# New orders of work in five places: a linear-attention and expert-mixture kernel on one core

## The chip, the cores and the metric

The kernel runs on one core of one Trainium2 chip. A core has TensorE (PE: matmuls, with its weight loads shown apart as PEld), VectorE (DVE), ScalarE (ACT), GpSimd (POOL) and SyncE (SP). The engines run side by side, each in the order of its own list of instructions, and wait for one another through semaphores. In this kernel POOL issues the loads from the inputs, and SP issues transposing DMAs, stores and reloads. The metric is the device time of the whole program in microseconds, as the median of several runs. For this kernel a difference of under 0.2% can't be told from none.

## The reference

Inputs are q, k, v (8 batches, 8 heads, 576 positions, 64 features) and a layer of 8 experts over 4608 tokens of 512 features.

```python
# attention, per batch and head
r = maximum(x, 0); phi(x) = concat(r * cos(pi/2 * pos/S), r * sin(pi/2 * pos/S))
kv = phi(k)^T @ v;  z = sum over positions of phi(k)
x = (phi(q) @ kv) / (phi(q) @ z + 1e-6)          # tokens x 512
# routing: 8 rounds of Sinkhorn on exp(x @ w_gate - max)
P /= P.sum(1) + 1e-9;  P /= P.sum(0) + 1e-9;  P *= N / E
# experts
out = sum over e of P[:, e] * (maximum(x @ w1[e], 0) @ w2[e])
```

All tokens go through all experts, so the work is almost all matmuls: x by w1 (512 x 1024) and the hidden layer by w2 (1024 x 512), eight times.

## The kernel before, in words

**Two phases.** In the first, attention of batch after batch is made in between the matmuls of expert 0. In the second, experts 1 to 7 run over six units of 768 tokens each (two halves of 384), with Strassen's scheme of seven products for both layers.

**The written order.** `te`, `ve` and `se` (class `InOrder`) tie each instruction of TensorE, VectorE and ScalarE to the one issued before it on the same engine, so that these engines follow the program's text. From the end of the first unit on `ve`, and from expert 2 on `se`, is the free engine, and the scheduler may move what is not tied.

**First phase.** Expert 0 works in blocks `j` of 512 tokens with 16 slots each: slots 0 to 7 are `ffn1` (one of eight column tiles of w1, four matmuls of 512 columns), slots 8 to 15 are halves of `ffn2`. The table `todo`, filled by `at(block, slot, fn, ...)`, says which attention step stands behind which slot. Block `j` carries attention of batch `j + 1` and the preparing of batch `j + 2`. A batch has four head pairs `hk`, loaded in two halves:
- `load`: q, k, v from memory, on POOL's queue;
- `prep_q`: q times cos and sin on VectorE; for batches 0 and 1 `turn` transposes it on TensorE, from batch 2 on a transposing DMA on SP does;
- `prep_k` is the Relu of k, `prep_kp` its product with cos and sin, `prep_v` the copy of v beside a column for z;
- `sums` makes kv and z on TensorE and copies them out; `denominators` makes the divisors and, on VectorE, their reciprocals `hl`;
- `spread_out` (copies `rb` on ACT) and `numerators` (products on VectorE) write `xT`; `attend` is both;
- `gates` makes exp of the routing logits, `P_tok`.

Batch 0 has no expert work beside it: it is written out by hand ahead of the blocks, with `keep_busy` matmuls on constants as fillers. It ends in the first four column tiles of block 0, whose four k tiles are interleaved with the attention's head pairs.

**Between the phases.** Blocks 7 and 8 of expert 0 have no attention. There the Sinkhorn rounds are made by the generator `sinkhorn`, five steps per round: row sums and reciprocal; scaling and column sums `colp`; two of the expert's weight sums (`tw_steps`); a matmul of `colp` with ones on TensorE and further weight sums; reciprocal and scaling. `balanced(n)` takes n steps. Beside it VectorE makes `x_sums`, the Strassen sums of x for a unit (S1, S2, S4 and one in place in `xT`), which are also saved to memory so that later experts reload them with `x_again`. The last block's `ffn2` (`dealt`) is spread as fillers over the first unit of expert 1 (`start_fill`), together with Sinkhorn's last rounds.

**Second phase.** `group` makes one of four column groups of a unit: seven products, with copies on ACT (`Y`, u2, u4, Relu) and additions on VectorE between them, and a call of `fill` behind each. In later units `pair_fill` puts one step of the second layer (`Pair`) there; it also issues `gate`, ScalarE's scaling of one finished tile of expert 0 by its P, for the 36 tiles one by one.

Of the kernel before, what the change touches and what calls it, by code (L numbers as in the profile page):

```python
# [25 lines left out]
def kernel(  # L26
# [128 lines left out]
    def ffn2(hT, w, c0, g, y_ps, fts):  # L155

        for ft in fts:
            te.matmul(
                out=y_ps,
                lhsT=hT[:, ft, c0 : c0 + P],  # L160
                rhs=w[1][:, ft, :],
                start=(ft == 0),
                stop=(ft == FT - 1),
            )
        if FT - 1 in fts:

            if g % 2 == 0 or g < (B - 1) * TCH // P:
                se.copy(out=acc(g), in_=y_ps)
            else:
                ve.tensor_copy(out=acc(g), in_=y_ps)  # L170

    def store(g, cols=slice(0, Dm), queues=(nc.sync, nc.sync)):
        for half, queue in enumerate(queues):
# [5 lines left out]
            )  # L179

    with ExitStack() as p1:
# [13 lines left out]
        landing = {}  # L195
        sources = {"q": q, "k": k, "v": v}

        def load(b, half, names="qkv", held_back=False):
            for name in names:
# [6 lines left out]
                if held_back:  # L206
# [10 lines left out]
        load(0, 0, "q")  # L217
        gidx = cs_pool.tile([P, C], FP32, name="gidx")
# [4 lines left out]

        ones_sq = cs_pool.tile([P, P], F16, name="ones_sq")
# [6 lines left out]
        load(0, 1, "q")  # L231
        for name in "kv":
            load(0, 0, name)
            load(0, 1, name)
# [22 lines left out]
        for _ in range(74):  # L257
            keep_busy(1)
# [17 lines left out]
        for hh in range(2):  # L276
            ve.tensor_copy(
                out=cs_half[hh * HP : (hh + 1) * HP, :, :, hh],
                in_=cs[hh * HP : (hh + 1) * HP, :, :, 0],
            )  # L280
# [8 lines left out]
        C3 = C // 3  # L289

# [6 lines left out]
        with nc.allow_low_precision("sums of zeros and ones"):  # L297
# [11 lines left out]
        ones_col = const.tile([P, 1], FP32, name="ones_col")  # L309
        ve.memset(ones_col[:], 1.0)  # L310
        ones_all = const.tile([P, P], FP32, name="ones_all")
        ve.memset(ones_all[:], 1.0)
        eps_row = cs_pool.tile([1, 32], FP32, name="eps_row")
        ve.memset(eps_row[:], 1e-6 / XS)
# [8 lines left out]
        lent = acc_lo[:, G_LO - 4 : G_LO, :].rearrange("p g d -> p (g d)").bitcast(F16)  # L323
        VA = C * (D + 2)
        v_augs = [
            lent[:, i * VA : (i + 1) * VA].rearrange("p (c d) -> p c d", d=D + 2)
            for i in range(4)
        ]
# [7 lines left out]
        for t in v_augs:  # L336
            ve.memset(t[:, :, D : D + 1], 1.0 / XS)

# [7 lines left out]
        def prep_q(b, hk):  # L346
# [12 lines left out]
            if by_dma:  # L359
# [5 lines left out]
                if b == 3 and hk == 0:  # L365

                    after(landing["v", b, 1], turned)
            else:
# [77 lines left out]
        def sums_begun(b, half):  # L446
# [7 lines left out]
            kv_ps = [ps_s.tile([P, 512], FP32, name="small_ps") for hh in range(2)]  # L454
# [157 lines left out]
        for hk in range(HK):  # L612
            if hk == 3:
# [3 lines left out]
                prep_q(0, hk)  # L617
                key_sums_made(0, z_ps)
            else:
                prep_q(0, hk)  # L620
            for i in range(3):
                turn(0, hk, i, True)
                keep_busy(3)
        prep_kp(0, 0)
        prep_kp(0, 1)
        denominators(0, range(0, 4))
        keep_busy(8)
        for hk in (2, 3):
            prep_k(0, hk)
        z_ps = key_sums(1)  # L630
        prep_kp(0, 2)
        key_sums_made(1, z_ps)
        prep_kp(0, 3)
        keep_busy(5)
        denominators(0, range(4, 8))
        for half in range(2):
            sums_made(0, half, sums_begun(0, half))
            keep_busy((0, 18)[half])
# [6 lines left out]
        ]  # L645
        for hk in range(HK):
            attend(0, hk)
            for kt in ((), (0,), (1,), (2, 3))[hk]:
                for ft, h_ps in enumerate(first_ps):
                    te.matmul(  # L650
                        out=h_ps[:],
                        lhsT=w0[0][:, kt, ft * P : (ft + 1) * P],
                        rhs=xT[:, kt, 0:TCH],
                        start=(kt == 0),
                        stop=(kt == KT - 1),
                    )
                    if kt == KT - 1:
                        se.activation(out=hT[:, ft, 0:TCH], in_=h_ps[:], func=AF.Relu)
            for i in ((), (0,), (1, 2), ())[hk]:
                prep_k(1, i, i < 2)  # L660
            for i in ((), (0,), (1,), (2, 3))[hk]:
                if i == 3:
                    prep_k(1, i, False)
                prep_kp(1, i)
# [3 lines left out]
        for j in range(B):  # L668
            b = j + 1
            if j == 0:  # L670
# [4 lines left out]
                for hk in range(HK):  # L675
                    for i in range(3):
                        at(0, (5, 6, 6, 7)[hk], turn, 1, hk, i, i != 1)
                    if hk == 0:
                        at(0, 5, prep_q, 1, 3)
                    if hk == 2:  # L680
                        at(0, 6, prep_v, 1, 0, se.copy)
                        at(0, 6, prep_v, 1, 2, ve.tensor_copy)
                    if hk == 3:
                        at(0, 7, prep_v, 1, 1, se.copy)
                        at(0, 7, prep_v, 1, 3, ve.tensor_copy)
# [6 lines left out]
            elif b < B:  # L692
# [14 lines left out]
                elif j == 2:  # L707
                    at(j, 0, sums, b, 1)
# [5 lines left out]
                at(j, 6 if j == 1 else 3 if j == 2 else 4, denominators, b)  # L714
# [567 lines left out]
```

The softmax here doesn't subtract the row's maximum and nothing guards it: scores larger than these inputs give would overflow.

## Time and profile before

| what | us |
|---|---|
| median of 4 runs (977.34 to 979.83) | 978.69 |
| the profiled execution | 977.77 |
| its span, first to last instruction | 976.1 |
| TensorE, VectorE, ScalarE busy | 961.7, 807.9, 564.0 |
| end of batch 0 and first products of block 0 | 24.9 |
| block 1; block 2; blocks 3 to 6 | 44.8; 65.4; 84.5 to 162.1 |
| blocks 7 and 8; first unit of expert 1 | 162.1 to 184.7; to 205.3 |

Times inside the profile are microseconds from the span's start. A line of the timeline has the start, the time, the engine, the line of code, the operation with what it writes and reads, its size and its count, and in brackets how long the engine stood idle before it and for whom. Instructions that were recorded by the helper of `InOrder` all show its line, L109, so they are told apart by the tiles they write. The page shows the granted clock of TensorE as 9 tenths or more in all of its 40 slices.

### The profile page before, as it was taken

To read this page: it belongs to the slowest core of one execution; us is meant where nothing else is said; L and a number is where in the kernel's file an instruction comes from. 1 tells how busy PE (TensorE), PEld (TensorE's weight loads), DVE (VectorE), ACT (ScalarE), POOL (GpSimd) and SP (SyncE) were. 2 spreads that over 40 slices of the span, in tenths; PEclk is the share of its full clock that TensorE was granted. 3 is DMA by queue.
4 is the path that set the end of the run, shared out by engine and by line. 5 is a ranking of instruction groups with operands and counts; after the bars stand their busy time and mean duration, and the time that the engine had idled before them with its cause. 6 is when DMAs were issued, how large, how long until landed. Compare 5 with 4: busy or idle time off the path is not lost.

```text
span 976.1 us, 20236 instructions
## 1 busy us (share of the span) xinstructions
PE 961.7 (99%) x7855; PEld 674.9 (69%) x7855; DVE 807.9 (83%) x1833; ACT 564.0 (58%) x1262; POOL 60.7 (6%) x82
## 2 busy tenths in 40 slices
PE   9999999999999999999999999999999999999997
PEld 6545555457777777777777777777777777777775
DVE  7767775888988987987888987987888887988887
ACT  5766665477776555555555555555555555555551
POOL 6231110010000000000000000000000000000001
PEclk9999999999999999999999999999999999999999
DMA  9999985331104401332103401323103401104435
GB/s 163 188 156 168 158 136 111 68 68 39 37 26 84 77 25 42 66 55 65 33 26 85 77 25 42 63 55 67 34 26 83 78 25 40 35 26 122 126 89 128
DMA packets 80336, 73.54 MB, mean 75 GB/s; under 512 B 33264, under 2 KB 72176, under 8 KB 80240
## 3 DMA queue, kind: packets, MB, share of 16 engines
q0 software_dynamic: 27232, 30.94, 20.4%
q1 hardware_dynamic: 52768, 41.06, 17.3%
q8 instruction: 61, 1.00, 0.4%
q14 instruction: 35, 0.29, 0.1%
q10 hardware_dynamic: 240, 0.26, 0.1%
HBM read 83.12 MB, written 12.98 MB: 98 GB/s over the span
## 4 chain that ended last, share of the span: by engine, by line
PE 88%; DMA 4%; DVE 3%; issue 2%; ACT 1%; POOL 1%; POOLq 0%; ACTq 0%; SPq 0%
PE rows_ps L109 33%; PE h_ps L109 26%; PE p_ps L109 11%; PE copied_ps L109 11%; PE y_ps L109 4%; PE small_ps L109 2%; DMA k_ld<-in_k_dram 1%; DMA w2e<-in_moe_w_dram 1%; DMA w1e<-in_moe_w_dram 1%; DMA acc_hi<-q_p 1%; DVE P_tok L109 1%; DVE colp L109 0%; POOL q_ld L202 0%; DVE rs L109 0%; DVE acc_hi L955 0%
## 5 line engine op out<-in xcount | busy, mean ns | idle before, releaser
L955 DVE SCALAR_TENSOR_TENSOR acc_lo<-rows_ps,P_tok,acc_lo 128x512 f32<-128x512 f32 (+1 forms) x322 | 203.6, 641 | 74.8 <-PE rows_ps L109 74.8
L109 PEld LDWEIGHTS <-H 128*128 128x128 f16 x2080 | 203.1, 98 | 82.5 <-issue 1.2
L891 ACT CAST u<-h_ps 128x384 f16<-128x384 f32 x288 | 137.8, 478 | 131.2 <-PE h_ps L109 131.2
L109 PEld LDWEIGHTS <-w1e 128*128 128x128 f16 x1632 | 157.7, 98 | 67.6 <-issue 5.2
L885 DVE CUSTOM_DVE_ANT_0 H<-p_ps,u 128x384 f16<-128x384 f32 x329 | 181.5, 552 | 6.5 <-PE p_ps L109 6.5
L109 PEld LDWEIGHTS <-hs 128*128 128x128 f16 x1500 | 146.6, 98 | 56.2
L109 PE MATMUL h_ps<-S,w1e 128*128 128x384 f16 x672 | 164.1, 326 | 0.7 <-ACT u L109 0.6
L109 PE MATMUL p_ps<-xT,T 128*128 128x384 f16 x672 | 164.1, 326 | 0.1
L109 PE MATMUL rows_ps<-V,H 128*128 128x256 f16 x1000 | 150.0, 273 | 0.7 <-DVE acc_hi L955 0.7
L109 PE MATMUL rows_ps<-w2e,hs 128*128 128x256 f16 x1000 | 150.0, 273 | 0.0
L109 PE MATMUL h_ps<-xT,w1e 128*128 128x384 f16 (+1 forms) x616 | 148.7, 350 | 0.1
L923 ACT ACTIVATE H<-h_ps 128x384 f16<-128x384 f32 x144 | 70.7, 491 | 95.0 <-PE h_ps L109 95.0
L109 PEld LDWEIGHTS <-T 128*128 128x128 f16 x1008 | 98.4, 98 | 30.1 <-issue 3.6
L109 PE MATMUL rows_ps<-w2e,H 128*128 128x256 f16 (+1 forms) x568 | 92.3, 284 | 0.0
L904 ACT COPY copied_ps<-h_ps 128x384 f32<-128x384 f32 x144 | 67.5, 468 | 35.4 <-PE h_ps L109 35.4
L914 ACT ACTIVATE H<-copied_ps 128x384 f16<-128x384 f32 x144 | 70.9, 492 | 20.3 <-PE copied_ps L109 20.3
L109 PE MATMUL h_ps<-S,T 128*128 128x384 f16 x336 | 81.8, 324 | 0.4 <-ACT copied_ps L109 0.3
L109 PE MATMUL copied_ps<-xT,w1e 128*128 128x384 f16 x336 | 82.1, 326 | 0.0
L109 PE MATMUL copied_ps<-w2e,H 128*128 128x256 f16 x504 | 75.5, 272 | 0.0
L109 PE MATMUL rows_ps<-V,hs 128*128 128x256 f16 x500 | 75.0, 272 | 0.0
L955 DVE SCALAR_TENSOR_TENSOR acc_lo<-copied_ps,P_tok,acc_lo 128x256 f32<-128x256 f32 x126 | 60.3, 478 | 0.6 <-PE copied_ps L109 0.2
L955 DVE SCALAR_TENSOR_TENSOR acc_hi<-rows_ps,P_tok,acc_hi 128x512 f32<-128x512 f32 (+1 forms) x56 | 41.4, 738 | 20.5 <-PE rows_ps L109 19.7
(145 smaller groups left out, 948.8 us busy)
## 6 DMA issues: line engine op xcount, KB each, us to landing
S<-x_saved SPq DMA_DIRECT2D x108, 192.0 KB, 2.4
out_dram<-acc_lo SPq DMA_DIRECT2D x62, 128.0 KB, 2.4
w1e<-in_moe_w_dram POOLq DMA_DIRECT2D x7, 1024.0 KB, 8.7
w2e<-in_moe_w_dram POOLq DMA_DIRECT2D x7, 1024.0 KB, 10.0
q_ld<-in_q_dram POOLq DMA_DIRECT2D x16, 288.0 KB, 6.5
k_ld<-in_k_dram POOLq DMA_DIRECT2D x16, 288.0 KB, 8.2
v_ld<-in_v_dram POOLq DMA_DIRECT2D x16, 288.0 KB, 9.2
x_saved<-S SPq DMA_DIRECT2D x18, 192.0 KB, 1.9
```

Source lines behind the costliest of these rows:

```text
L109: i = getattr(self.engine, name)(*args, **kwargs)
L885: latest = ve._custom_dve(TENSOR_ADD_SAT, out=out, in0=ps[:, 0:TU], in1=t[:], s0=FP32_MAX, s1=0.0)
L891: se.copy(out=t[:], in_=ps[:, 0:TU])
L904: se.copy(out=Y[:, 0:TU], in_=X[:, 0:TU])
L914: se.activation(out=h11, in_=Y[:, 0:TU], func=AF.Relu)
L923: se.activation(out=h12, in_=X[:, 0:TU], func=AF.Relu)
L955: ve.scalar_tensor_tensor(out=a, in0=rows, scalar=P_tok[:, g, self.e : self.e + 1], in1=a, op0=ALU.mult, op1=ALU.add,)
```

## The change

Five edits:
1. **First batch in new order.** The second q load is issued ahead of the position table (iota), k's first half ahead of the identity; small constants are written earlier. The 74 fillers of 128 columns at the start become 110 of 64. All four `prep_q` come before k; `cs_half` is filled after the second; sums, spreads and numerators are written out one by one, the second sums in another bank; the first products follow; k of batch 1 is prepared behind them instead of in between. In block 0 the turns of batch 1 move from slots 5, 6, 6, 7 to 6, 6, 7, 7, and all copies of v go to VectorE.
2. **Fourth batch's sums later.** Batch 3's preparing in block 1 and its sums and denominators take the slots that later batches have: sums in block 2, slot 2 (before: block 1 slot 15 and block 2 slot 0). All its transposes wait for its last v load, and the loads of batch 4 wait for its last transpose. Batch 4's preparing in block 2 is one slot later.
3. **x sums of two units in block 6.** They go into k's and q's buffers at slots 2 and 5, are saved, and are reloaded with `x_again` at the start of the second phase.
4. **Sinkhorn on a table of slots.** The steps of the rounds stand at listed slots and fills; the weight sums are dealt 2, 3, 4, 3, 4 to the rounds; block 7's tiles are all copied by ScalarE; the last block's second layer goes in 8 parts per tile, one in each fill, the last two in the second unit.
5. **Gating in ScalarE's order.** `gate` uses the ordered engine also after expert 1.

```diff
-            if g % 2 == 0 or g < (B - 1) * TCH // P:
+            if g % 2 == 0 or g < B * TCH // P:
                 se.copy(out=acc(g), in_=y_ps)
...
+    def x_sums(n, ts):
...
+        for i, t in enumerate(ts):
+            saved.append(
+                nc.sync.dma_start(out=x_saved[n, i], in_=t.rearrange("p k t -> p (k t)"))
+            )
...
+                if behind is not None:
+                    after(turnings[behind], i)
+                elif held_back:
                     after(ve.last, i)
...
         load(0, 0, "q")
+        load(0, 1, "q")
         gidx = cs_pool.tile([P, C], FP32, name="gidx")
...
+        load(0, 0, "k")
...
-        load(0, 1, "q")
-        for name in "kv":
-            load(0, 0, name)
-            load(0, 1, name)
+        load(0, 1, "k")
+        for half in range(2):
+            load(0, half, "v")
...
-        for _ in range(74):
-            keep_busy(1)
+        for _ in range(110):
+            te.matmul(
+                out=idle_ps[:, 0:HP], lhsT=ones_sq[:],
...
-                if b == 3 and hk == 0:
+                if b == 3:
                     after(landing["v", b, 1], turned)
+                turnings[b, hk] = turned
...
         for hk in range(HK):
+            prep_q(0, hk)
+            if hk == 1:
+                halve()
             if hk == 3:
                 prep_k(0, 0)
                 prep_k(0, 1)
                 z_ps = key_sums(0)
-                prep_q(0, hk)
-                key_sums_made(0, z_ps)
...
+        sums_made(0, 0, sums_begun(0, 0))
+        keep_busy(20)
+        spread_out(0, 0)
+        numerators(0, 0)
+        keep_busy(4)
+        spread_out(0, 1)
+        sums_made(0, 1, sums_begun(0, 1, (ps_h[0], "h_ps")))
...
+        numerators(0, 1)
+        spread_out(0, 2)
+        first_l1(0, (2, 3, 0, 1))
+        numerators(0, 2)
+        spread_out(0, 3)
+        first_l1(1, range(4))
+        numerators(0, 3)
+        prep_k(1, 0)
+        prep_k(1, 1)
+        first_l1(2, range(4))
+        first_l1(3, range(4))
         for hk in range(HK):
-            attend(0, hk)
...
+            if hk >= 2:
+                prep_k(1, hk, False)
+            prep_kp(1, hk)
...
-                        at(0, (5, 6, 6, 7)[hk], turn, 1, hk, i, i != 1)
+                        at(0, (6, 6, 7, 7)[hk], turn, 1, hk, i, i != 1)
...
-                elif j == 2:
-                    at(j, 0, sums, b, 1)
...
-                    (4, prep_q, 0), (5, prep_q, 1), (8, prep_k, 0), (8, prep_q, 2),
-                    (9, prep_k, 1), (10, prep_kv, 0), (10, prep_k, 2), (12, prep_q, 3),
-                    (12, prep_kv, 1), (12, prep_k, 3), (13, prep_kv, 2), (14, prep_kp, 3),
-                    (14, prep_v, 3),
+                    (4, prep_q, 0), (5, prep_q, 1), (9, prep_k, 0), (8, prep_q, 2),
+                    (10, prep_k, 1), (12, prep_q, 3), (12, prep_k, 2), (13, prep_k, 3),
+                    (13, prep_kv, 0), (14, prep_kv, 1),
                 ) if j == 1 else (
-                    (4, prep_q, 0), (5, prep_k, 0), (5, prep_q, 1), (6, prep_k, 1),
-                    (8, prep_q, 2), (8, prep_k, 2), (10, prep_q, 3), (10, prep_k, 3),
+                    (5, prep_q, 0), (6, prep_q, 1), (8, prep_k, 0), (8, prep_q, 2),
+                    (9, prep_k, 1), (10, prep_q, 3), (10, prep_k, 2), (11, prep_k, 3),
                     (11, prep_kv, 0), (14, prep_kv, 1),
...
-                if j == 1:
-                    at(j, 15, sums, b + 1, 0)
             if j == 1:
                 for name in "qkv":
                     for half in range(2):
-                        at(j, 12, load, b + 2, half, name, True)
+                        at(j, 12, load, b + 2, half, name, True, (b + 1, HK - 1))
...
+        for n in range(2):
+            at(B - 2, (2, 5)[n], x_sums_early, n)
...
-            se.mul(out=acc(g), in_=acc(g), mul=P_tok[:, g, 0:1])
+            bound[2].mul(out=acc(g), in_=acc(g), mul=P_tok[:, g, 0:1])
...
+    tw_steps = [[steps_left.pop(0) for _ in range(n)] for n in (2, 3, 4, 3, 4, 0, 0, 0)]
...
+    for n in range(2):
+        x_again(n, xs_first[n], saved[-1])
...
-            2 if j < NJ - 1 else 4,
+            2 if j < NJ - 1 else 8,
...
-            since = (j - B + 1) * NS + slot - 5
-            if since == -4:
-                balanced(3)
-            elif since >= 0 and since % 5 < 2:
-                balanced((1, 4)[since % 5])
+            balanced({1: 3, 4: 5, 8: 5, 13: 5, 17: 5, 22: 5}.get((j - B + 1) * NS + slot, 0))
...
-        if k_fill % 7 in (0, 2, 3, 5):
+        for _ in range(1 + (k_fill % 14 == 1)):
             next(tiles, None)
-        if k_fill % 6 != 1:
-            balanced(1)
+        balanced({3: 1, 4: 1, 6: 1, 8: 2, 12: 1, 13: 1, 15: 1, 17: 2, 21: 1, 22: 1}.get(k_fill, 0))
...
     def pair_fill():
         nonlocal k_fill, slot2
         k_fill += 1
+        for _ in range(2):
+            next(tiles, None)
```

## The prediction

> **What bounds the kernel now.** I read the page first, for which engine is never idle; then busy time by stage, for where TensorE stops being full; then TensorE's waits and its timeline in those stages; then the engine each wait names.
>
> ```profile
> PE 961.7 (99%) x7855; PEld 674.9 (69%) x7855; DVE 807.9 (83%) x1833; ACT 564.0 (58%) x1262; POOL 60.7 (6%) x82
> ...
> 44.80:65.40 20.60, 20.28 (x213) 9.77 (x213) 17.11 (x38) 14.49 (x32) 4.30 (x6) 1.00 1.02 149
> 65.40:84.50 19.10, 17.87 (x198) 9.23 (x198) 12.27 (x29) 12.49 (x29) 5.47 (x8) 1.00 1.16 187
> 84.50:162.10 77.60, 77.60 (x834) 40.17 (x833) 53.86 (x123) 48.41 (x113) 13.41 (x19) 1.00 0.88 144
> 162.10:184.70 22.60, 22.57 (x127) 10.77 (x126) 17.86 (x47) 10.90 (x20) 0.00 (x0) 1.00 0.15 53
> 184.70:205.30 20.60, 17.31 (x93) 8.73 (x92) 15.59 (x37) 12.01 (x25) 3.87 (x3) 1.00 0.31 52
> 308.70:400.00 91.30, 91.30 (x701) 68.30 (x699) 76.87 (x170) 51.04 (x115) 0.88 (x1) 1.00 0.20 45
> ```
>
> The columns are PE, PEld, DVE, ACT, POOL, clock, DMA share, GB/s. TensorE bounds the kernel, so nothing can be gained where it is full: from 84.5 to 162 and after 308. Busy time hides short stops, because matmuls overlap; so I measure a stop as start to next start, less what the same matmuls take undisturbed (0.216 us for 512 columns, 0.163 for 384). From 308 to 955 that excess is about 0.01 us per 10 us. It is found in four places before that: the first 35 us, blocks 1 and 2 (56 to 73), the Sinkhorn stretch (176 to 200), and the unit behind it (200 to 210). The change touches all four.
>
> ```profile
> PE copied_ps L109 <- DVE colp L109: 3.0, 4, 1.2
> PE h_ps L109 <- ACT u L109: 0.6, 2, 0.3
> PE h_ps L109 <- ACT copied_ps L109: 0.3, 1, 0.3
> ```
>
> **Sinkhorn on a table of slots (-4.3).** Eight times a small product of column sums stands in TensorE's order and waits for VectorE's `colp`:
>
> ```profile
> 184.99 0.59 PE L109 MATMUL rows_ps<-w2e,H 128*128 128x512 f16 x2
> 186.78 0.39 PE L109 MATMUL copied_ps<-colp,ones_all 128*128 128x8 f32 x2 [1.19 <-DVE colp L109]
> 187.03 0.48 PE L109 MATMUL h_ps<-S,T 128*128 128x384 f16 x2
> ```
>
> Two matmuls of 0.43 take 1.79 here: 1.36 lost. By the same subtraction the third to eighth products lose 0.19, 0.14, 1.36, 0.47, 0.91 and 0.90, which is 3.97; and each of these six takes 0.24 where the two unhurried ones take 0.14, so 0.6 more. Loss: 4.6.
>
> One iteration costs VectorE, from the rows between 168.13 and 170.94 (reciprocal, scale, row sums, reciprocal, scale, column sums), 2.81; with 0.32 from the product to the reciprocal it can repeat every 3.2 us. Before, it is slower because VectorE's order also holds four weight sums (about 0.25 each), rows copies (0.69) and the x sums of two units (four of 0.55 each). The table puts the products of blocks 7 and 8 after slots 4, 8, 13, 17 and 22: 4 or 5 slots of 4 x 0.216, so 3.6 us or more. Between slot 22 and fill 3 stand one slot, the mark and 11 matmuls: 0.87 + 0.22 + 2.07 + 0.14 = 3.3. After that 9 fills of 0.54 (two of 384 columns, one of 512), so 4.9. All are over 3.2, the third by only 0.1. The weight sums now fall into the gaps left by the wider slots; the first two stand at slot 1 (166), and their weights, issued at 147.74, land 8.2 us later, so in time. Block 7's copies go to ACT, which was idle 1.13 and 3.00 us before the two it had (171.6, 175.2). Eight parts, two left for the next unit and other banks are the same matmuls: 0. One matmul per fill leaves 0.76 us between two accumulations in a bank; the copy between 190.98 and 191.75 fits that without a stop. I keep 0.3 for the narrow gap: -4.3. Ends: -4.6, and -1 if VectorE still comes half a microsecond late seven times.
>
> **x sums in block 6 (0).** Two times four additions of 0.56, 2.2 us each, go to VectorE at slots 2 and 5. VectorE is busy 53.86 of 77.60 in blocks 3 to 6, and 3.1 us idle before the numerators at 160.25. After the sums (147.1 on this trace) the first ends at 149.5, before the denominators' 149.8; the second runs from 152.3 to 154.5, before the numerators at 155.1. Uncovered it would cost 0.3 to 1.5. New DMA: six stores and six loads of 192 KB on SP (1.9 to 2.4 us each, 0.15 DMA share in that stage), needed first at 185. Behind them on SP nothing is due.
>
> **Gates in ScalarE's order (-0.6).** Four gates of expert 2's unit were free to move, and landed here, between the copies that TensorE waits for:
>
> ```profile
> 202.15 0.73 ACT L1107 ACTIVATE acc_lo<-acc_lo,P_tok 128x512 f32<-128x512 f32 x1
> 203.19 0.72 ACT L1107 ACTIVATE acc_hi<-acc_hi,P_tok 128x512 f32<-128x512 f32 x1
> ```
>
> TensorE loses 0.21, 0.44, 0.44, 0.46 and 0.11 from 201.8 to 210, 1.66 in all. In the new order they are gone from there; one copy of 0.59 now stands before the copy of h_ps in the second group, which I price at 0.3. So -1.35. But the order lists three of the four together in expert 2's first group, between the copy of h_ps and u2: 3 x 0.64 start to start, so u2 is ready at 3.05 us behind the first product where TensorE wants it at 2.3 to 2.75. That is +0.3 to +0.75; I take 0.75. The 0.35 us that each later unit of expert 1 loses has the same gates behind it and stays. Ends: -1.7 and +0.8.
>
> **Fourth batch later (-2.4).**
>
> ```profile
> 58.43 0.46 PE L109 MATMUL small_ps<-hl,acc_hi 96*128 96x192 f16 x3 [0.19 <-ACT rb L109]
> ...
> 67.38 0.46 PE L109 MATMUL small_ps<-acc_lo,k_p 64*128 64x65 f16 x18 [0.31 <-DVE acc_lo L109]
> 68.04 0.46 PE L109 MATMUL small_ps<-acc_lo,k_p 64*128 64x65 f16 x18 [0.21 <-DVE k_p L109]
> ...
> 72.52 0.34 PE L109 MATMUL small_ps<-acc_hi,zsel 128*32 128x192 f16 x6 [0.71 <-DMA acc_hi<-q_p]
> ```
>
> The first stop (0.35 + 0.29) is ACT standing in order on a Relu of k that waits for its load (idle 1.33 before 56.84); the Relu moves one slot back, behind the rb copies. The next two (0.48 + 0.37) are the fourth batch's sums, asked for before VectorE has made k_p and v; they go to slot 2 of block 2. The last (0.88) is a transposing DMA issued at 65.92, while the next batch's loads were issued from 65.87 on; it landed after 6.6 us, where (4,3) took 3.3. Sum 2.37. As a check, block 2 then has the written order of blocks 3 to 6, whose period is 19.0 without stops.
>
> New waits: the four transposes wait for the last v load (63.0; about 60.4 without transposes among the loads and with the shift below). Behind them on SP stand only transposes; for them waits TensorE's denominator product at 69.5. One each 1.35 us from 60.4, the last landing by 68.5: in time. The six loads of batch 4 then wait for that landing; behind them on POOL stand only later loads. Issue at 68.1, first landing 4.7 later (as 83.34 to 88.10), then 1.45 each: 72.8 to 80. VectorE wants the first at about 73, since its use moves from slot 4 to 5.
> A rule weighed here: the Trainium skill, "DMA: Bandwidth & Descriptors", section on queues, rings and completion order, has each engine go round its queues packet by packet. By it, holding loads back gains no bandwidth and only shifts them, 2.2 us later: with no slack at 73 that is +2 against -0.9, a net of -0.4 here. By the row, 6.6 against 3.3, the transpose gets its 3.3 back and the loads run 1.45 apart, undisturbed. I go by the row, and keep -0.4 as the end.
>
> **First batch in new order (-0.8).**
>
> ```profile
> 10.86 0.76 DVE L109 TENSOR_TENSOR q_p<-q_ld,acc_hi 128x1152 f16<-128x1152 f16 x1
> 12.02 1.42 DVE L109 TENSOR_TENSOR k_p<-k_ld,acc_hi 128x1152 f16<-128x1152 f16 x2
> 15.45 1.35 DVE L109 RECIPROCAL den<-y_ps 96x192 f32<-96x192 f32 x1
> 18.49 0.82 DVE L109 TENSOR_TENSOR xT<-small_ps,rb 128x384 f16<-128x384 f32 x2 [0.94 <-ACT rb L109]
> ```
>
> POOL: the second q load moves ahead of iota (issue 2.62 to 2.07), the tables 0.8 later (4.29 to 5.05), still before VectorE's 6.0. Landings run one per 1.45 from 8.94 on, so the stream gains 0.3. From k's landing (10.4) to the reciprocal VectorE ran 5.05: now the fourth q_p (0.7) fills the wait for k, and one k_p (0.7) goes behind, so the reciprocal starts at 14.2 and hl ends at 16.4 for 17.54. Spreads, products and copies follow as before with the second sums (0.6) among them: first products of block 0 end at 23.9 for 24.91. But the k_p that filled VectorE's waits between now come after: from 22.85 on 9.5 us of VectorE work without a gap (four k_p of 0.68, two Relu 0.33, four q_p 0.69, four turns 0.5, four v copies 0.37) to 32.4, and the sums end at 32.9 for 33.72. Fillers stand in TensorE's waits only: 0. So -0.8, and VectorE and the transposes carry it on. Ends: -2 (no refilled waits), +0.5 (w2, which lands until 34.25, or another wait takes it).
> The second rule: the Trainium skill, "TensorE: Matmul & The Clock Gate", Part 1, warns of half clock after an idle window of about 3.4 us. The trace shows the start alone: 74 fillers of 128 columns took 6.36 us, 107 ns apart and later 56. With 110 of 64 columns, half of each row's spacing, that is 5.3 us. The longest stop in my order is 0.9 (before hl), so by the row 0; by the rule too, unless a stop passes 3.4: then 3.4 us at half speed, +1.7.
>
> **Sum.** -0.8 - 2.4 + 0 - 4.3 - 0.6 = -8.1. The span 976.1 becomes 968.0; its execution took 977.77, 1.67 more, so 969.7; the runs' median, 978.69, lies 0.92 higher: 970.6, say 970.5.
>
> **Rivals.** (a) VectorE still comes last in Sinkhorn. For it: 0.1 of slack in one gap and 83% busy; against: the x sums and copies have left. 978.7 - (8.1 - 3.5) = 974. (b) The stops only change place: gates in expert 2 at +0.8, loads at their bad end, narrow slots, no gain at the start. 978. (c) Slower: batch 4's loads. They may not start until the fourth transpose lands, and transposes have taken 6.4 us (44.74 to 51.13). VectorE stands in order on the first q with the numerators of batch 3 behind it, and TensorE behind those. Each microsecond later than 73 costs one; from about 83 (landing of the last transpose at 78 instead of 68.5) it eats the other gains of 5.7 and the 2.4 too, and at 86 gives 981.5. For it: a DMA share near 1 in this stage; against: no load is in flight beside the transposes now.
>
> **How the numbers follow.** The forecast 970.5 has 0.74; its own range, from the ends of its terms taken half way, is 968 to 973. (a) has 0.13, (b) 0.05, (c) 0.08. A measurement tells 0.2% from nothing, 2 us here: faster 0.87, same 0.05, slower 0.08. The range 967.5 to 975 holds the forecast's case and most of (a).
>
> **What would show it.** The product behind colp without a wait, eight times, two products 3.2 us apart or more; no gate between 195 and 205, three together in expert 2's first group with one stop under 0.8; blocks 1 and 2 without waits on acc_lo, k_p or a transpose, and unit starts all earlier by about 3 at 75 and 8 at 215. It is wrong if TensorE waits for a load near 73, if `colp` is named again, or if the first sums do not end before 33.5.

## The result: 2.6 us faster, where 8.1 were forecast

| | before | after |
|---|---|---|
| median, us | 978.56 (53 runs) | 975.99 (32 runs) |
| the profiled execution; its span | 977.77; 976.1 | 976.55; 974.8 |

The ratio after to before is 0.9971, 95% interval 0.9963 to 0.9979. The sign was right, the size was not: 976.0 lies above the range of 967.5 to 975.

The busy time by stage of the changed kernel, cut where its blocks now begin (columns as in the prediction: PE, PEld, DVE, ACT, POOL, clock, DMA share, GB/s):

```profile
43.80:64.30 20.50, 20.11 (x210) 9.63 (x209) 14.29 (x33) 14.15 (x31) 4.30 (x6) 1.00 1.03 142
64.30:85.70 21.40, 19.36 (x205) 9.93 (x204) 13.33 (x30) 12.77 (x29) 4.31 (x6) 1.00 1.02 147
85.70:107.60 21.90, 19.56 (x210) 10.04 (x209) 17.75 (x40) 12.62 (x29) 6.98 (x10) 1.00 1.00 169
107.60:164.50 56.90, 56.90 (x618) 29.51 (x617) 41.58 (x94) 35.80 (x83) 7.60 (x11) 1.00 0.88 154
164.50:187.10 22.60, 22.60 (x131) 11.39 (x130) 17.15 (x48) 12.54 (x22) 0.25 (x1) 1.00 0.28 72
187.10:204.80 17.70, 17.50 (x102) 9.87 (x101) 13.82 (x30) 11.29 (x25) 4.07 (x4) 1.00 0.43 83
```

Sinkhorn's stretch, which had TensorE idle for 3.3 of 20.6 us, is full but for 0.2. Block 2 has TensorE idle for 2.0 us where it was 1.2, and block 3, which was full, for 2.3. Where the same matmul stands in both profiles, start against start:

| the same matmul | before | after | after less before | change of it | forecast |
|---|---|---|---|---|---|
| block 1 begins | 44.79 | 43.77 | -1.02 | -1.02 (first batch) | -0.8 |
| block 7 begins | 162.13 | 164.48 | +2.35 | **+3.37** (fourth batch) | **-2.4** |
| expert 1, second unit, second group: product for Y | 211.86 | 209.81 | -2.05 | -4.40 (Sinkhorn, and gates leaving) | -4.3 - 1.35 |
| expert 2, first unit, second group: product for Y | 304.54 | 303.23 | -1.31 | +0.74 (gates arriving) | +0.75 |
| end of the span | 976.1 | 974.8 | -1.3 | 0 | 0 |

So one term has the wrong sign and makes 5.8 us of the error, and a second, the gates leaving, won next to nothing.

Who TensorE waits for in blocks 1 to 3 (us in total, times, longest), after:

```profile
PE h_ps L109 <- DVE xT L109: 3.0, 3, 1.7
PE small_ps L109 <- DVE acc_lo L109: 1.3, 3, 0.6
PE small_ps L109 <- DVE hl L109: 0.4, 1, 0.4
```

The transpose's wait (`acc_hi<-q_p`, 0.7) is gone, as I had said, and the waits for VectorE are larger. The same view of VectorE from 55 to 95, before and then after:

```profile
DVE q_p L109 <- DMA q_pT<-q_p: 0.6, 1, 0.6
```

```profile
DVE q_p L109 <- DMA q_pT<-q_p: 7.4, 2, 4.8
```

VectorE waits for a transposing DMA before it makes a q_p. A q_p does not read a transpose; it overwrites a buffer that one still reads. `qp_pool` has three buffers and a batch has four head pairs. The timeline of VectorE, of POOL and SP, and of TensorE at this place, after:

```profile
80.64 0.30 DVE L109 TENSOR_SCALAR q_ld<-q_ld 128x576 f16<-128x576 f16 x1
85.76 0.76 DVE L109 TENSOR_TENSOR q_p<-q_ld,acc_hi 128x1152 f16<-128x1152 f16 x1 [4.82 <-DMA q_pT<-q_p]
...
87.47 1.54 DVE L109 TENSOR_TENSOR xT<-small_ps,rb 128x384 f16<-128x384 f32 x4
```

```profile
69.44 1.43 POOL L234 DMA_DIRECT2D q_ld<-in_q_dram  x2 [15.91 <-DMA acc_hi<-q_p]
...
77.05 10.80 SPq L403 DMA_TRANSPOSE q_pT<-q_p  x4
```

```profile
85.73 0.59 PE L109 MATMUL h_ps<-xT,w1e 128*128 128x512 f16 x2
88.07 0.38 PE L109 MATMUL h_ps<-xT,w1e 128*128 128x512 f16 x1 [1.74 <-DVE xT L109]
```

Batch 4's loads, held behind batch 3's last transpose, are issued at 69.44 (before: 65.87) and land from 73.8 to 83.2 (before: 71.1 to 80.0). At 77.05 batch 4's own transposes begin, in the middle of them; before they began at 76.45, at the loads' end. From issue to landing the transposes whose issue lies in 76 to 86 took, before and after:

```profile
DMA to landing us min/median/max: 3.3/4.2/4.8
```

```profile
DMA to landing us min/median/max: 4.3/6.8/8.6
```

The first lands at 85.7, and only then may VectorE make the fourth q_p; behind it in VectorE's order stand the numerators, for which TensorE waits. The same chain, a batch earlier and shorter, makes the stops at 64 to 70: all transposes of batch 3 now wait for the last v load (first issue 61.34), VectorE stands 2.59 us, and `xT` and the v copies come late.

### The profile page after: what moved, and what is told of

It reads as the page before. It is cut to its first block, busy times and chain, and to the rows that moved or that the text cites. A ratio compares the mean times of both kernels' runs of the same rounds, so it can differ in the third digit from the quotient of the medians.

```text
span 974.8 us, 20319 instructions
## 1 busy us (share of the span) xinstructions
PE 959.5 (98%) x7886; PEld 674.0 (69%) x7886; DVE 808.5 (83%) x1834; ACT 564.6 (58%) x1261; POOL 60.4 (6%) x82
## 4 chain that ended last, share of the span: by engine, by line
PE 90%; DMA 4%; DVE 3%; issue 2%; POOL 1%; ACT 0%; DVEq 0%; POOLq 0%; SPq 0%; ACTq 0%
PE rows_ps L109 34%; PE h_ps L109 27%; PE p_ps L109 11%; PE copied_ps L109 11%; PE y_ps L109 4%; PE small_ps L109 2%; DMA w1e<-in_moe_w_dram 1%; DMA w2e<-in_moe_w_dram 1%; DMA q_ld<-in_q_dram 1%; DMA k_ld<-in_k_dram 1%; DVE k_p L109 1%; DMA q_pT<-q_p 0%; DVE acc_hi L991 0%; DVE acc_lo L109 0%; POOL hs_last L1006 0%
## 5 line engine op out<-in xcount | busy, mean ns | idle before, releaser
L109 PEld LDWEIGHTS <-w1e 128*128 128x128 f16 x1632 | 157.9, 98 | 71.1 <-issue 9.4
L109 PE MATMUL rows_ps<-w2e,H 128*128 128x256 f16 (+1 forms) x568 | 94.4, 285 | 0.0
```

The source lines that it names most:

```text
L109: i = getattr(self.engine, name)(*args, **kwargs)
```

## The experiments

Where nothing else is said, a kernel is the changed one with the edit shown. The kernel before, measured beside each, stood at 978.5 to 979.2. "Lent" is memory of accumulators that are not yet in use, in place of a buffer of `qp_pool`.

### Which part of the fourth batch's edit costs

All of it undone (slots, sums, waits, holds):

> The changed kernel with all of the fourth batch's edit undone: its slots, its sums, its transposes and the loads behind them as in the kernel before. Read from the two traces the edit costs 3.4 us (1.0 us ahead at block 1, 2.35 us behind at block 7), for the 2.4 us gain of the prediction. Theory: 972.6 us. As predicted: 978.4 us.

973.23 us, ratio 0.993 (0.9905 to 0.9954). The edit costs 2.8 us by the medians. What is left of my sum without it is -5.7, that is 973.0: the other four terms together come out, though one of them, the gates, does not by itself (below).

Only the hold of the loads taken away:

```diff
-  at(j, 12, load, b + 2, half, name, True, (b + 1, HK - 1))
+  at(j, 12, load, b + 2, half, name, True)
```

> The changed kernel; only the loads of batch 4 no longer wait for the last transpose of batch 3, but for VectorE's place in the order, as before. Theory (the buffer): they are issued near 66 for 69.4, land by 79.5, the transposes of batch 4 land before 81 and TensorE's stop at 86 to 92 (2.5 us) is gone; the one at 65 to 70 stays, and batch 3's last transpose gets its share of the loads' packets again (0.7 us near 72): 974.2 us. Rival (the slots): 976 to 977, since only the contention comes back.

973.65 us, 0.9939 (0.9918 to 0.9959). And only the hold put into the kernel with the edit undone:

> The changed kernel with the slots, sums and transposes of the fourth batch as in the kernel before, and only the loads of batch 4 held behind the last transpose of batch 3. Theory (the hold alone makes the loss): the loads are issued near 69.3 in place of 65.6, land by 82.5 among the transposes of batch 4, VectorE waits 4 us or more for q_pT<-q_p near 81 and TensorE 2.5 to 4 us for xT near 85, against 0.6 us that the last transpose of batch 3 wins: 975.5 to 977, which is 2.3 to 3.8 us over the same kernel without the hold (973.2). If TensorE stands over 3.6 us there, its clock is halved behind it, as with one transpose ahead of the loads, and 1.9 us come on top. Rival (the slots and the transposes behind the v load do it together with the hold): under 974.5.

976.58 us, 0.998 (0.9969 to 0.9992), 3.35 more than without. The size was as expected, the place was not: in the old slots ScalarE's Relu of k comes sooner, ScalarE stood 4.06 us for `k_ld`, and TensorE waited for its `hT` (2.1 us the longest) and `rb` at 77 to 81. Late loads reach TensorE by whichever engine stands in order on them first. Both together: **the hold makes the loss** (2.3 us in the new slots, 3.4 in the old). The slots and the other waits lose 0.4 without the hold and gain 0.6 with it, by the medians, which is less than each kernel's runs scatter.

Then the wait of the transposes alone, as before:

```diff
-                if b == 3:
+                if b == 3 and hk == 0:
                     after(landing["v", b, 1], turned)
```

> The changed kernel; only the first transpose of batch 3 waits for its last v load, as in the kernel before; the loads of batch 4 still wait for the last transpose. Theory (the buffer): one transpose goes ahead of the loads and has landed by 62, so the first wait of VectorE is gone (2.3 us of TensorE), and the three that are left land 1.4 us sooner, which gives the loads of batch 4 and its transposes 1.4 us: 972.3 us. Rival (the slots): 975.5 to 976.

976.45 us: a miss. The first stop fell from 1.11 to 0.33, but the others stayed, the last transpose was issued at 65.46 (65.69 in the changed kernel), the loads at 69.25, and VectorE, there sooner, waited 6.7 us in place of 4.8. The longer stop had a price of its own, which the stages show:

```profile
84.00:88.00 4.00, 0.92 (x5) 0.29 (x3) 1.74 (x4) 0.59 (x1) 0.00 (x0) 1.00 1.08 160
88.00:89.00 1.00, 0.38 (x1) 0.10 (x1) 1.00 (x4) 0.00 (x0) 0.65 (x1) 1.00 0.76 151
89.00:93.00 4.00, 3.71 (x9) 1.12 (x8) 3.59 (x8) 1.20 (x2) 3.63 (x6) 0.57 0.97 142
```

After 3.65 us without work the granted clock fell to 0.57, and nine matmuls took 3.72 us where the changed kernel's nine take 2.07: 1.65 us more.

### Is it the buffer?

```diff
+            if b in (3, 4) and hk == 3:
+                q_p = acc_lo[:, 18 + 2 * b : 20 + 2 * b, :].rearrange("p g d -> p (g d)").bitcast(
+                    F16
+                )[:, 0 : C * 2 * D].rearrange("p (c a d) -> p c a d", a=2, d=D)
+            else:
+                q_p = qp_pool.tile([P, C, 2, D], F16, name="q_p")
```

> The changed kernel; only q_p of the fourth head pair of batches 3 and 4 goes into memory lent from the accumulators of later tokens, so VectorE needs no buffer that a transpose still reads. Theory (the buffer): VectorE's two waits for q_pT<-q_p, 2.6 us near 62 and 4.8 us near 81, are gone though the transposes are as late as before, and with them TensorE's stops for xT and acc_lo at 65 to 70 (2.3 us) and 86 to 92 (2.5 us): 971.2 us. Rival (the slots: VectorE has too much to do between the later slots): no wait of VectorE matters, 975.5 to 976. Rival (the loads of batch 4 are late for VectorE): VectorE then waits for q_ld or k_ld instead, 975 or more.

984.07 us, 1.005 (1.004 to 1.006). The first half came out as expected: both waits of VectorE for `q_pT<-q_p` are gone, and 64 to 70 has no stop for `xT`. The second half did not. VectorE now starts batch 5's loads at 84.66, ahead of batch 4's last transpose at 86.64, and the waits of TensorE are

```profile
PE small_ps L109 <- DMA q_pT<-acc_lo: 8.9, 1, 8.9
PE small_ps L109 <- DVE xT L109: 1.4, 1, 1.4
```

with, for that one transpose,

```profile
DMA to landing us min/median/max: 14.5/14.5/14.5
```

So the buffer is how the late transpose reached TensorE, and it had also kept the next loads away from it. Without it the transpose is later still, and the denominators wait for it directly.

Lent memory for batch 3 alone, loads not held:

> The changed kernel without the hold of batch 4's loads, and with q_p of batch 3's fourth head pair in memory lent from the accumulators of later tokens. Theory (the buffer): VectorE's wait of 1.9 us near 62 is gone, with it TensorE's stops of 0.42, 0.69 and 0.73 at 65 to 70: 973.65 less 1.84, 971.8 us. Rival: VectorE that is early starts the loads of batch 4 early (they follow its place in the order), so they fall among batch 3's transposes, and the denominators wait for those at 70: 973 us or more.

983.37 us; the rival given there came true. VectorE, 1.9 us sooner, started the loads at 62.78, among batch 3's transposes:

```profile
PE small_ps L109 <- DMA q_pT<-q_p: 6.1, 1, 6.1
PE small_ps L109 <- DMA acc_lo<-q_p: 2.9, 1, 2.9
```

### Is there a window for the loads?

```diff
-  at(j, 12, load, b + 2, half, name, True, (b + 1, HK - 1))
+  at(j, 12, load, b + 2, half, name, True, (b + 1, 1))
```

> The changed kernel; the loads of batch 4 wait for the second transpose of batch 3 in place of the last. Theory (there is a window: loads and transposes share the DMA engines, so the six loads must stream between batch 3's transposes, which are through by 69, and batch 4's, which begin at 77): the second transpose lands near 66, the loads are issued there (with the hold on the last: 69.4; without: 65.4), their packets come behind batch 3's transposes and end by 80. VectorE's wait near 81 falls from 4.8 to under 2.5 us, TensorE's at 86 to under 0.5: 973.7 us, as without the hold. Rival (any hold does harm, for the loads' own sake): 975 or more.

973.65 us, 0.9949 (0.9934 to 0.9964) as expected; its four runs lie within 1 us (973.12 to 974.08), where the 32 of the changed kernel spread over 5.5. Issued at 66.07, nearly as early as before (65.87), the loads land by 79.1 and block 3 is full. It is not the hold that does harm but its length: 3.4 us.

The same with lent memory for batch 3; then for 3 and 4; then also with batch 5's loads behind the third transpose of batch 4 (and q_p of batch 5 lent); then also batch 6's:

> As before this one (loads of batch 4 behind the second transpose), and q_p of batch 3's fourth head pair in lent memory. With the loads free this made 983.4, since VectorE came early and started the loads at 62.8, among the transposes of batch 3. Theory: held by the second transpose they start near 65.5 again, so this time only the stops of 0.42, 0.69 and 0.73 at 65 to 70 go: 971.9 us. Rival (the lent memory itself does harm): 975 or more.

> The changed kernel with the loads of batch 4 behind the second transpose, and q_p of the fourth head pair in lent memory for batches 3 and 4 both. If VectorE's wait for a buffer is the only way in which late transposes of batch 4 cost time, the 5.0 us wait near 79 and TensorE's 2.04, 0.51 and 0.40 at 83 to 90 go: 970.7 us, and that is where the predicted gain lies. If the DMA engines set the pace of this stage, the gain goes on to the next place: VectorE then starts batch 5's loads sooner, they fall among batch 4's last transposes, and TensorE waits for q_pT in the denominators near 90: 973 us or more.

> The changed kernel with q_p of the fourth head pair in lent memory for batches 3, 4 and 5; the loads of batch 4 behind the second transpose of batch 3, and those of batch 5 behind the third of batch 4, all q first. Theory (loads and transposes must not meet, and then the stops are gone): batch 4's transposes are through by 86, batch 5's loads are issued near 85 and stream from 89 to 98, TensorE's 6 to 7 us at 89 to 97 are not there: 970.7 us. Rival (the DMA engines have no room left, 8.7 us of loads and 5.6 us of transposes with 3.3 to 4.6 us before the first landing of each in every block of 19): the wait goes to batch 5's transposes, among the end of its own loads, or VectorE waits for the third q_p's load near 93: 973 us or more.

> As the one before, and the loads of batch 6 likewise behind the third transpose of batch 5. If the next place at which loads and transposes meet is batch 6's loads, started by an early VectorE, this one has 970.7 us where the one before has 973 or more. If both have it, batch 6's loads come late enough by themselves. If both are at 973 or more, the DMA engines set the pace.

973.59, 980.36, 977.50 and 980.83 us. In the first the stops at 64 to 70 went (the span from block 1 to block 3 is 2.45 us shorter than without lent memory), and block 3 lost 2.04 + 0.51 + 0.40, for batch 4's transposes now began at 74.6, among loads that ended at 80.8. In the second that went too, and the denominators of batch 4 waited:

```profile
PE small_ps L109 <- DMA q_pT<-q_p: 6.2, 1, 6.2
PE small_ps L109 <- DMA q_pT<-acc_lo: 1.2, 1, 1.2
```

In the third and fourth TensorE waited 4.1 and 5.5 us for `hT`, as ScalarE stood 5.3 and 6.8 us on a k whose load, held back, now came behind both q. In all four, what was won at one place was lost at a later one: at transposes among loads in the first two, at a late load in the last two. The DMA share of blocks 1 and 2 is 1.0 or more before and after. I had expected 971.9 for the first and 970.7 for the other three, and was wrong each time; for those three the rival, 973 or more, came true. That no order at all could win the 2.4 us is not shown.

The edit alone on the kernel before, so with block 1 a microsecond later:

> The kernel before with the fourth batch's edit alone. If the edit itself makes the loss, and not that the first batch's edit brings TensorE to block 1 a microsecond sooner: 978.6 + 2.8, 981 to 982 us, with VectorE waiting for q_pT<-q_p near 64 and near 83. If it needs the sooner start: 979.5 or less. As predicted for this edit: 976.2.

980.27 us, 1.0009 (0.9996 to 1.0021): no gain, and at most a small loss, 1.6 us by the medians where it is 2.8 in the changed kernel. That lies between the two cases that I had named. Batch 4's transposes begin at 78.42 in place of 77.05 while its loads end at nearly the same time (83.6 for 83.2), and VectorE waits 3.3 us for 4.8. By these two traces the microsecond that the first batch wins makes the collision worse; no run varies it alone.

### Sinkhorn and the gates

Sinkhorn's table with the x sums, alone on the kernel before:

> The kernel before with Sinkhorn on the table of slots, the tiles that go with it, and the x sums of two units in block 6; the first batch, the fourth batch and the gates as before. As predicted for these two edits: -4.3, 974.4 us. From the traces (4.65 us between 164.5 and 201.8, with part of the gates' loss behind it): 973.6 to 974.2. Rival (VectorE stays last): 976 or more, with waits for colp.

974.47 us, 0.9962 (0.9951 to 0.9973). In the profiles, block 7's start to the end is 976.1 - 162.13 = 814.0 before and 972.7 - 163.01 = 809.7 here: -4.3, the forecast. In the changed kernel all eight products of column sums stand without a wait; the last three read

```profile
188.72 0.28 PE L109 MATMUL copied_ps<-colp,ones_all 128*128 128x8 f32 x2
...
194.09 0.28 PE L109 MATMUL copied_ps<-colp,ones_all 128*128 128x8 f32 x2
...
199.31 0.28 PE L109 MATMUL copied_ps<-colp,ones_all 128*128 128x8 f32 x2
```

with nothing in brackets, and 0.28 for two where they took 0.39 with the wait.

The gates free again:

```diff
-            bound[2].mul(out=acc(g), in_=acc(g), mul=P_tok[:, g, 0:1])
+            se.mul(out=acc(g), in_=acc(g), mul=P_tok[:, g, 0:1])
```

> The changed kernel with the gates of expert 2 free to move again, as in the kernel before. As predicted: the edit wins 1.35 between 201 and 210 and loses 0.75 in expert 2's first group, so without it 976.6 us. Theory from the traces: between 199 and 208 VectorE has work without a gap and TensorE meets it at 207.4 in any case (0.9 us), so the four gates that come back there cost little that is not lost anyway, and the 0.74 at 290 to 300 is gone: 975.4 us.

975.49 us, 0.9965 (0.9952 to 0.9979), not to be told from the changed kernel by its median. Runs whose mean granted clock was 0.999 or 1.0 tell more: five of the ten here, 973.98 to 974.73, against 24 of the 32 of the changed kernel, 974.20 to 977.19. Among those the free gates are 1.1 us faster by the medians (974.5 and 975.6). The profiles agree: in the unit behind Sinkhorn this kernel waits as the kernel before did,

```profile
204.44 0.48 PE L109 MATMUL h_ps<-S,w1e 128*128 128x384 f16 x2 [0.26 <-ACT u L109]
...
209.22 0.48 PE L109 MATMUL h_ps<-S,w1e 128*128 128x384 f16 x2 [0.83 <-ACT u L109]
```

and loses 0.42 + 0.22 + 0.99 = 1.63. The changed kernel has no gate there and loses 0.21 + 0.25 + 1.02 = 1.48:

```profile
208.29 0.48 PE L109 MATMUL p_ps<-xT,T 128*128 128x384 f16 x2 [0.85 <-DVE H L921]
```

```profile
205.49 0.68 DVE L1023 TENSOR_TENSOR V<-w2e 128x1024 f16<-128x1024 f16 x1
206.08 0.41 DVE L1006 TENSOR_TENSOR hs<-H 128x512 f16<-128x512 f16 x1
206.42 0.68 DVE L1024 TENSOR_TENSOR V<-V,w2e 128x1024 f16<-128x1024 f16 x1
207.02 0.41 DVE L1006 TENSOR_TENSOR H<-H 128x512 f16<-128x512 f16 x1
207.35 0.42 DVE L1006 TENSOR_TENSOR hs<-hs,H 128x512 f16<-128x512 f16 x1
207.69 0.55 DVE L921 CUSTOM_DVE_ANT_0 H<-p_ps,u 128x384 f16<-128x384 f32 x1
```

VectorE is the next in line. And in expert 2's first group the three gates between the copy and u2 stand as forecast, for 0.74 us:

```profile
296.74 0.72 ACT L109 ACTIVATE acc_lo<-acc_lo,P_tok 128x512 f32<-128x512 f32 x1
297.36 0.71 ACT L109 ACTIVATE acc_hi<-acc_hi,P_tok 128x512 f32<-128x512 f32 x1
297.97 0.71 ACT L109 ACTIVATE acc_lo<-acc_lo,P_tok 128x512 f32<-128x512 f32 x1
298.58 0.46 ACT L927 CAST u<-h_ps 128x384 f16<-128x384 f32 x1
```

Taking those gates off ScalarE (to GpSimd), with lent memory for two batches:

> As the one before, with the four gates of expert 2's first unit on GpSimd. TensorE's 0.74 in expert 2's first group goes; its stop near 207 stays at 0.85 to 1.0, as VectorE makes it: 0.7 under the one before.

The loss in expert 2 went (-0.74 between the two profiles), but the stop near 207 grew from 0.9 to 1.3 and the whole took 981.44 for 980.36, which the scatter of the stage ahead (979.1 to 983.2) covers. The longer stop has an entry in the trace: while GpSimd scaled tiles, one of VectorE's sums of V ahead of the stop took 1.10 us in place of 0.68.

Two combinations on the hold behind the second transpose and lent memory for batch 3: gates free, and the last tile's copy taken off VectorE with the gates on GpSimd:

> As the one before (loads behind the second transpose, lent memory for one q_p), and the gates of expert 2 free to move. 971.9 less what the free gates won in the run of the changed kernel with them (0.5 by the medians, 0.9 by the profiles behind 165): 971.0 to 971.4 us. If the edit of the gates wins as predicted, 972.5.

> As the one with the loads behind the second transpose and one q_p in lent memory, with the gates in ScalarE's order, but the four of expert 2's first unit on GpSimd, and the last tile of expert 0 copied by ScalarE in place of VectorE (0.68 us of VectorE's work ahead of TensorE's stop at 207.4). If VectorE's work without a gap makes that stop, it falls from 0.85 to 0.25, and the 0.74 in expert 2's first group goes: 971.9 - 1.3 = 970.6 us. If the copy only moves the wait to ScalarE (u2 behind it): 971.2 or more.

974.74 and 974.79 us. Both lost more in block 3 (2.5 and 2.7 us in place of 2.0), and in the first's profile the granted clock was 0.50 for 3.41 us behind it. In the second the copy's 0.68 us was filled at once: VectorE is no longer in written order there, the scheduler put V's third sum (0.68) ahead of the addition, one addition took 0.82 us for 0.41 while GpSimd scaled its tiles, and the stop was 1.3, not 0.25. So these two runs do not show what the gates on GpSimd would give without that delay; its cause was not looked into.

The best: both doubtful edits undone, the first batch, the x sums and Sinkhorn kept.

> The changed kernel with the fourth batch's edit and the gates' edit undone: what is left are the first batch, the x sums and Sinkhorn. By the profiles behind block 7 the gates' edit costs 0.3 to 0.9 us: 973.2 less 0.5, 972.7 us, the best so far. If the gates' edit wins as predicted: 973.8.

973.04 us, 0.994 (0.9918 to 0.9962): faster than both kernels, and with 973.23 for the ordered gates no difference between those two is shown. Its runs spread from 971.7 to 977.1, and the profiled one, at 977.09, shows what the fourth batch's edit had been about:

```profile
PE small_ps L109 <- DMA acc_hi<-q_p: 3.4, 1, 3.4
```

Batch 3's last transpose among batch 4's loads, 3.4 us in this execution and 0.5 to 1.0 in others of this order. The loads behind the second transpose, at 973.65 and within 1 us in four runs, are as fast, and by these few runs steadier.

## Why the prediction was right or wrong, step by step

- **First batch (-0.8): right.** First products ended at 23.9 as said, the sums at 32.7 (said: 32.9), block 1 came 1.02 sooner. No run has this edit alone, but block 1 begins at 43.2 to 44.0 in every profile with it and at 44.8 to 45.3 in the three without.
- **Sinkhorn (-4.3): right**, by the run that has it alone. The narrow gap cost nothing that a wait shows.
- **x sums in block 6 (0): right.** Blocks 4 to 6 are full (56.90 of 56.90).
- **Gates (-0.6): wrong.** The 0.75 in expert 2 was right (0.74). The step that failed is the -1.35 for the stretch from 201.8 to 210: I priced what left ScalarE and did not ask who comes next. VectorE's work without a gap does, and the gain is 0.15. By the spans behind block 7 the edit costs 0.2 (without the fourth batch's edit) to 0.9 us (with it).
- **Fourth batch (-2.4): wrong, and the cause of the miss.** It failed in "New waits", in two sentences. Of the transposes behind the v load I wrote that behind them stand only transposes and that TensorE's denominators wait for them; VectorE waits too, through the third buffer of q_p, and the numerators with it. This put new stops at 64 to 70 (1.11 + 0.69 + 0.73) in the place of the 2.37 that went; with the buffer lent and the loads behind the second transpose they were gone. Of the loads I followed the first landing to VectorE: 72.8 forecast, 73.8 measured, wanted at 75.9, so that slack was there. I did not follow the last landing (80 forecast, 83.2 measured) to batch 4's transposes at 77. This brought 1.90 + 0.51 + 0.40. So 2.53 and 2.81 came for 2.37, 3.0 of the measured 3.37; most of the rest is a stop for `hl` at 56 (0.39 idle).
- **The rule weighed there.** From the Trainium skill, "DMA: Bandwidth & Descriptors", section on queues, rings and completion order, I had that each DMA engine goes round its queues packet by packet, and took from it that holding loads back wins no bandwidth and only shifts them. I went by the row (6.6 against 3.3) instead. The row was right for the transposes that the hold frees; the rule was right about the rest: the collision was shifted from batch 3's transposes to batch 4's. It also gives an estimate of the size. The DMA rows of the changed kernel between 40 and 112 are

```profile
q0 software_dynamic: 5961, 6.46, 60.2%
q1 hardware_dynamic: 18944, 4.72, 43.3%
```

(packets, MB, share of 16 engines): 1084 bytes a packet for the loads, 249 for the transposes. A transpose of 288 KB has 1184 of these packets. If the two queues take turns packet for packet as the profile counts them, which no run shows by itself, as many of the loads' packets pass beside it: 4.3 loads or 6.3 us at 1.45 each. With the 3.3 us that a transpose takes alone that is an estimate of 9.6 us. 8.6 was measured for the first of batch 4, which had four loads still to land beside it. The 14.5 and 14.9 measured beside six loads, behind an earlier transpose still in flight, are more than the estimate gives.
- **Rival (c)** named the hold, its place and the resource, and gave it 0.08. Its path was not the one that came (VectorE on the first q), and its argument against, that no load is in flight beside the transposes, held for batch 3 alone. For batch 4 the trace before already showed the meeting: its first two transposes, issued at 76.45 and 78.11, took 4.65 and 4.78 us beside loads that landed until 79.96, where the one issued at 82.07 took 3.25. Rival (b), stops that change place, is what became of two of the five terms.

## What to carry to other kernels

When a transfer is held back, follow its last landing as well as its first, and look for what starts on the same DMA engines in between, the same batch's next step included. When a wait moves to an instruction that frees a buffer, count the buffers and list who writes the next one. And where a stop is to go from a stretch in which two engines are busy without a gap, or the DMA share is 1, price the gain at what the next in line leaves of it.

## What the runs showed of the hardware

**A transpose beside loads starves, and its queue with it.** Alone it took 3.2 to 3.4 us from issue to landing, beside loads 8.6 and 6.8 for the first two of batch 4 in the changed kernel, and up to 14.9 in other runs. SyncE itself is held up: its issue took 1.3 us alone and up to 7.9 and 8.1 beside loads.

**TensorE's clock halves in mid-kernel, and the length of the stop alone does not decide it.** In the run with free gates a stop of 2.27 us, with one of 0.35 close behind it, was enough; in the second combination one of 2.50 with 0.35 behind it was not:

```profile
86.07:89.48 3.41, 0.79 (x4) 0.23 (x3) 3.09 (x7) 0.55 (x1) 0.99 (x2) 1.00 0.91 193
89.48:92.89 3.41, 3.41 (x9) 1.10 (x8) 3.24 (x7) 1.19 (x2) 3.31 (x5) 0.50 0.95 129
```

```profile
81.89:85.30 3.41, 2.30 (x12) 0.96 (x11) 0.92 (x2) 0.63 (x2) 0.00 (x0) 1.00 0.96 122
85.30:88.71 3.41, 1.67 (x7) 0.67 (x7) 3.41 (x9) 0.61 (x2) 2.24 (x4) 1.00 0.72 122
```

The windows are not chosen freely. In the 20 traces of this case, twelve stretches at a clock of 0.50 lie between 10 us and the last products. Each lasts 3.41 us or two, three or four times that, and where a trace has two they start a multiple of 3.41 us apart (96.53 and 120.42 in the last of the four runs on the window for the loads: seven times). So the clock changes on a fixed grid. Laid on the grid of its own trace, every one of the twelve begins behind a window in which TensorE was busy 0.44 of the time or less, and behind no window with 0.48 or more does one begin. The first stop above fell into one window, busy for 0.79 of 3.41 us; the second was cut in two by the boundary at 85.30. The stop of 1.74 us in the changed kernel left its window busy for 0.56. One such stretch costs half of 3.41, so 1.7 us; 1.65 was measured twice.

The Trainium skill, "TensorE: Matmul & The Clock Gate", Part 1, puts the window at about 3.4 us and says that it runs freely, so that the point of change varies; the traces agree, with 3.41. My prediction counted such a loss only from stops of 3.4 us on, and that was too late: a window did not have to be idle throughout. Where a stop falls on the grid differs from run to run, and this is much of the changed kernel's scatter: its 8 runs with a mean granted clock of 0.997 or 0.998 took 977.25 to 979.71 us, the other 24, at 0.999 or 1.0, 974.20 to 977.19.
